# Mirrored rows of the second mixture go through a scratch in tile order, reversed by DRAM-to-DRAM copies

## The chip, the core and the metric

The kernel runs on one core of a Trainium2 chip. The metric is the device time of one execution in microseconds (us). The kernel before takes 789.74 us, the median of 3 runs (789.72 to 790.67).

Its engines are called PE (matrix multiply; PEld is its weight load), DVE (vector), ACT (scalar), POOL and SP. SP computes nothing here: it issues DMA transfers, in the order of the program.

## The reference, cut to what matters

```python
x = attn(x)                      # rfft along the sequence, complex mix, soft threshold, irfft
x = x + relu(norm(x)*g @ w11) @ w12          # first MLP, row by row
X = np.fft.fft(np.fft.fft(x, axis=1), axis=2)
u = x + np.real(X)                           # second mixture
out = u + relu(norm(u) @ w21) @ w22          # second MLP, row by row
```

There are 2 sequences (b = 0, 1) of 3136 rows of 256 fp32 channels; the MLPs are 1024 wide. Because x is real, row 3136 - n of `real(X)` is row n with its channels reversed (channel 256 - c in place of c). So one computed tile serves two sets of rows, the rows n and their mirror.

## The kernel before, in words

3136 rows are split as 49 x 64: row n = k1 + 49 * a, with k1 below 49 and a below 64. The first stages write the first mixture to DRAM, and 13 chunks of up to 512 rows (`mlp1`, the loop `run_mlp`) turn it into `dX1` in DRAM. A stage of 49-point transforms (`Stage98`) reads `dX1` as `u0r` and writes `dA2`. The second MLP (`mlp2`) has 13 chunks again, in the order of `plan2`: a chunk holds two pairs, such as k1 = 4 and 3 of sequence 0, and a pair fills two tiles of 128 rows. The first tile is the rows of k1 in its upper 64 partitions and those of k1 - 1 in its lower 64. The second is the mirrored rows: rows 3136 - k1 and 3136 - k1 + 1, and from each of them 64 rows backwards in steps of 49. The front of a chunk (`Front.stage_b`, `dmix`) computes real(X) for the first tile and adds it, reversed in the channels, to the second (L901, L904).

The rows of x that the tiles add to are loaded by `Chunk.fetch` (L660, `yb<-dX`), three chunks ahead. The results are stored by `Chunk.store` (L811, `out_dram<-o`). For a pair there are two loads of 64 rows and one of 128 mirrored rows, and as many stores. The access pattern of the mirrored ones is built in `chunks2`: in memory it is 2 x 64 rows of 1 KB, with a step of minus 49 rows inside.

Between norm and matmul the rows are transposed. `flip` transposes 32x32 blocks on DVE (L713) and writes them to DRAM (L719, `dT<-q`); `land` reads them back in the other order (L727, `q<-dT`); `trans` splits what came into two parts on ACT and DVE (L200 and L208, `u0r<-q`). This round trip of the next chunk happens while the present chunk is multiplied: `land` is asked for after the fourth of eight first-layer blocks (`LAND_AT`), behind the last store of the chunk before (`sent`), and `trans` at the first tile of the second layer.

The order on each engine is fixed when the program is built. All transfers but one go through SP's queue. Each DMA tells of its landing on one of eight counters, taken in turn (DMAHW0 to DMAHW7 in the order below), and SP issues a DMA only once the one that is eight before it has landed; such a wait holds up all that stands behind it. PE writes the second layer into two banks (`psb`), and DVE (L801, L802) frees a bank by adding it to the rows.

The lines of the change are those that build the mirrored access pattern in `chunks2` and the hooks ahead of the two calls of `run_mlp`; hooks are keyed by chunk, layer ("l1" or "l2") and step.

Of the kernel before, what the change touches and what calls it, by code (L numbers as in the profile page):

```python
# [9 lines left out]
F32 = mybir.dt.float32  # L10
# [27 lines left out]
LATE = {"b": (4, 6), "mix": (6, 7), "stats": (("l1", 7), ("l2", 0)), "norm": (("l2", 0),) * 4, "flip": (("l2", 2), ("l2", 3))}  # L38
LAND_AT = ("l1", 3)
PAD_AT = (15, 17)  # L40
TRANS1_AT = (4, 6)
PREP0_AT = (23, 24, 26, 28)
L2_BEHIND = 7
# [10 lines left out]
NB = 2  # L54
N = 3136
N1 = 49
N2 = 64
D = 256
NQ = 98
NK = 24  # L60
# [100 lines left out]
def fourier_moe_kernel(ctx, tc, x, w_r, w_i, b_r, b_i, g_ln, w11, w12, w21, w22,  # L161
                       t_ca, t_cam, t_cim, t_cb, t_ci, t_cb0, t_ci0, t_cd, t_ident, out):
    nc = tc.nc
    sp = nc.sync
# [3 lines left out]
    dp = ctx.enter_context(tc.tile_pool(name="dp", bufs=1, space=bass.MemoryType.DRAM))  # L168
# [36 lines left out]
    mark, tab, spx = {}, {}, {}  # L205
# [18 lines left out]
    def scratch(nm, n=NQ):  # L224
        return [dp.tile([n, FW], F32, name=f"{nm}{b}") for b in range(NB)]

    dY = [dp.tile([2, NQ, FW // 2], F32, name=f"dY{b}") for b in range(NB)]
    dX1, dA2 = scratch("dX1", 128), scratch("dA2", 128)

    def by_k1(t, k1, n):  # L230

        v = t.rearrange("q f -> (q f)")
        return v[(k1 - 1) * 32768:(k1 - 1 + n) * 32768].rearrange("(k p c) -> p k c", k=n, c=D)
# [584 lines left out]
    def chunks1(b, wv):  # L818
        cs = []
        if b == 0:  # L820
            plan = [(c * 512, 4) for c in range(6)]
        else:
            plan = [(64, 2), (320, 3)] + [(704 + c * 512, 4) for c in range(4)] + [(2752, 3)]
        for r0, nt in plan:
            lo = [(ALLP, 0, nt, half_rows(dY[b], r0, 128, nt))]
            st = [(ALLP, 0, nt, rows(dX1[b], r0, 128, nt))]
            if b == 1 and r0 == 64:
                for src, lst in ((dY, lo), (dX1, st)):
                    for h, (bb, rr) in enumerate(((0, 3072), (1, 0))):
                        lst.append((slice(h * 64, h * 64 + 64), nt, 1, half_rows(dY[bb], rr, 64, 1) if src is dY  # L830
                                    else rows(src[bb], rr, 64, 1)[:, 0, :]))
                nt += 1
            cs.append(Chunk(nt, lo, st, wv, True))
        return cs
# [71 lines left out]
    def chunks2(plan, wv):  # L906
        cs = []
        for pairs in plan:
            lo, st, nt = [], [], 0
            for pr in pairs:  # L910
                for src, lst in ((dX1, lo), (out, st)):
                    for h, (b, k1) in enumerate(pr):
                        v = src[b] if src is out else src[b].rearrange("q (j c) -> (q j) c", c=D)[0:N]
                        lst.append((slice(h * 64, h * 64 + 64), nt, 1,
                                    v.rearrange("(k a) c -> k a c", a=N1)[:, k1, :]))
                    if pr[0][1]:
                        b, k1 = pr[0]
                        assert pr[1] == (b, k1 - 1)
                        v = src[b]
                        m = bass.AP(v.tensor, v.offset + (N - k1) * D, [[D, 2], [-N1 * D, N2], [1, D]])  # L920
                        lst.append((ALLP, nt + 1, 1, m))
                nt += 2 if pr[0][1] else 1
            cs.append(Chunk(nt, lo, st, wv, False, Front(pairs)))
        return cs
# [84 lines left out]
    def l_pad(b):  # L1009

        sp.dma_start(out=dX1[b][NQ:128].rearrange("q (k f) -> q k f", k=8), in_=x[b].rearrange("k q f -> q k f")[0:128 - NQ])

    for b in range(NB):
        todo.setdefault(PAD_AT[b], []).append(lambda b=b: l_pad(b))
    mlp1 = chunks1(0, wv1) + chunks1(1, wv1)
# [168 lines left out]
    plan2 += [[((1, 4 * i + 4), (1, 4 * i + 3)), ((1, 4 * i + 6), (1, 4 * i + 5))] for i in range(5)]  # L1184
    plan2 += [[((1, 24), (1, 23))]]
    mlp2 = chunks2(plan2, wv2)


# [7 lines left out]
    def after(k, i, f):  # L1196

        def g():
            with tc.issue_after(mlp1[k].rest[i]):
                f()  # L1200
        return g

    def in_turn(chunks, k, f):

        def g():
            with tc.issue_after(chunks[k].pe):
                f()
        return g
# [15 lines left out]
    def store3(n, cs):  # L1224

        def g():
            with tc.issue_after(mlp1[n].trip):
                for c in cs:
                    inv[1].store(c)
        return g  # L1230

    def hook(k, part, i, f):
        hooks.setdefault((k, part, i), []).append(f)

    mlp2_w = load_mlp(w21, w22, r2b, "stg", True)
    hook(3, "l1", 5, mlp2_w[0])
    for (k, i), f in zip(MLP2_AT, mlp2_w[1:]):
        hook(k, "l1", i, after(k, i, f))
    for c, i in enumerate(TRANS1_AT):
        hook(0, "l1", i, in_turn(mlp1, 0, lambda c=c: mlp1[1].trans(c)))  # L1240
# [4 lines left out]
    hook(0, "l1", 0, l_cd)  # L1245
    hook(2, "l1", 3, store3(3, range(2)))
    hook(2, "l2", 2, store3(4, range(2, 4)))
    hook(*STAGE4_FROM[0], s4[0].start)
    hook(8, "l1", 1, after(8, 1, s4[0].ahead))
    hook(8, "l1", 6, in_turn(mlp1, 8, s4[0].middle2))  # L1250
# [6 lines left out]
    def ahead1():  # L1257
        with tc.issue_after(mlp2[2].applied), tc.issue_after(mlp2[0].pe):
            s4[1].ahead()

    hook(*STAGE4_FROM[1], s4[1].start)
    hook(0, "l2", 2, ahead1)
    hook(1, "l1", 2, in_turn(mlp2, 1, s4[1].middle2))
# [38 lines left out]
```

## Time and profile before

| | us |
|---|---|
| median of 3 runs | 789.74 |
| profiled execution | 789.01 |
| its span, first to last instruction | 787.1 |
| PE busy | 771.3 |
| weight loads (PEld) busy | 642.6 |
| DVE busy | 545.7 |
| ACT busy | 359.7 |
| transfers of SP's queue, share of 16 DMA engines | 43.2% |

The profiled execution is one run under the hardware profiler; the time outside its span is 1.9 us. A busy share is an average over stages, so it says where to look and not what an edit is worth. PE is busy in 98% of the span; PE's clock is granted in full except in one stretch around 510 to 521 us. The kernel moves 43% of what its DMA engines have time for, so in the mean they are not the limit; a single transfer can still be late.

### The profile page before, as it was taken

The page shows a single profiled execution, that of the slowest core. Times are in us where ns is not written, and L with a number is a line of the kernel's source. Part 1 is how long each engine was busy: PE and PEld are TensorE (multiplying, and loading weights), DVE is VectorE, ACT ScalarE, POOL GpSimd, SP SyncE. Part 2 cuts the span into 40 slices and gives each one's busy share as a digit, 9 for nine tenths or more (in the row PEclk, how much of TensorE's full clock was granted, in tenths as well). Part 3 has the DMA queues.
Part 4 walks back from the last instruction along what each step waited for, and adds up shares of the span by engine and source line. Part 5 has one row for each costly group of instructions (what it writes and reads, how often), then busy time and mean ns, then how long its engine had stood idle before and what let it go on. Part 6 is the DMA issues. An engine that isn't in the chain of part 4 may idle for free.

```text
span 787.1 us, 12213 instructions
## 1 busy us (share of the span) xinstructions
PE 771.3 (98%) x4396; PEld 642.6 (82%) x4396; DVE 545.7 (69%) x1253; ACT 359.7 (46%) x791; POOL 104.4 (13%) x113
## 2 busy tenths in 40 slices
PE   9999999999999999999999999789999999999997
PEld 3989978976788889977778988567788898888886
DVE  6799986886757988668667866446646667666643
ACT  0543366365654535536343244346534535444421
POOL 0564321330111001100000001324000000000000
PEclk9999999999999999999999999979999999999999
DMA  8853202613084333577862326555543334422211
GB/s 235 260 173 125 81 1 55 221 54 108 30 280 132 135 121 94 137 198 214 248 176 67 121 89 159 154 169 159 165 135 99 105 121 122 113 68 74 62 33 41
DMA packets 84706, 101.02 MB, mean 128 GB/s; under 512 B 20306, under 2 KB 63036, under 8 KB 84450
## 3 DMA queue, kind: packets, MB, share of 16 engines
q1 hardware_dynamic: 84566, 100.18, 43.2%
q8 instruction: 35, 0.57, 0.3%
q14 instruction: 25, 0.20, 0.1%
q10 hardware_dynamic: 80, 0.07, 0.0%
HBM read 60.76 MB, written 41.42 MB: 130 GB/s over the span
## 4 chain that ended last, share of the span: by engine, by line
PE 88%; DMA 4%; DVE 4%; issue 1%; ACT 1%; SPq 1%; POOL 0%; DVEq 0%; POOLq 0%; ACTq 0%
PE psb L795 22%; PE psb L796 11%; PE psa L218 11%; PE psa L220 11%; PE psa L219 11%; PE psb L520 7%; PE psc L337 4%; DMA q<-dT 4%; PE psc L867 2%; PE psa L487 2%; PE psc L542 2%; PE psa L324 2%; PE psc L892 1%; DMA yb<-dX 1%; PE psc L933 1%
## 5 line engine op out<-in xcount | busy, mean ns | idle before, releaser
L774 ACT ACTIVATE h<-psa 128x512 fp32r<-128x512 f32 (+2 forms) x208 | 117.8, 572 | 213.6 <-PE psa L220 160.3
L776 DVE SCALAR_TENSOR_TENSOR h<-psa,h 128x512 fp32r<-128x512 f32 (+2 forms) x208 | 134.8, 653 | 63.9 <-ACT h L774 60.4
L795 PE MATMUL psb<-r2b,h 128*128 128x512 f32 x392 | 138.9, 401 | 7.8 <-DVE o L802 7.8
L795 PE MATMUL psb<-r3a,h 128*128 128x512 f32 x392 | 137.6, 397 | 0.0
L796 PE MATMUL psb<-r2b,h 128*128 128x256 f32 x392 | 106.8, 283 | 0.0
L796 PE MATMUL psb<-r3a,h 128*128 128x256 f32 x392 | 106.5, 280 | 0.0
L795 PEld LDWEIGHTS psb<-r2b,h 128*128 128x128 f32 x392 | 73.0, 191 | 24.2 <-issue 8.5
L795 PEld LDWEIGHTS psb<-r3a,h 128*128 128x128 f32 x392 | 72.1, 188 | 20.8 <-issue 5.7
L520 PE MATMUL psb<-wm,h 128*128 128x256 f32 (+1 forms) x600 | 84.4, 290 | 0.0
L218 PE MATMUL psa<-u0r,r2b 128*128 128x512 f32 (+2 forms) x208 | 82.0, 394 | 1.1 <-ACT u0r L200 1.1
L520 PEld LDWEIGHTS psb<-wm,h 128*128 128x128 f32 (+1 forms) x600 | 76.6, 188 | 5.0 <-issue 3.2
L218 PE MATMUL psa<-u0r,r3a 128*128 128x512 f32 (+1 forms) x208 | 80.5, 387 | 0.0
L219 PE MATMUL psa<-u0r,r2b 128*128 128x512 f32 (+2 forms) x208 | 78.7, 378 | 0.0
L219 PE MATMUL psa<-u0r,r3a 128*128 128x512 f32 (+1 forms) x208 | 78.7, 378 | 0.0
L220 PE MATMUL psa<-u0r,r2b 128*128 128x512 f32 (+2 forms) x208 | 78.2, 381 | 0.0
L796 PEld LDWEIGHTS psb<-r2b,h 128*128 128x128 f32 x392 | 75.2, 192 | 3.1
L220 PE MATMUL psa<-u0r,r3a 128*128 128x512 f32 (+1 forms) x208 | 76.4, 378 | 0.0
L796 PEld LDWEIGHTS psb<-r3a,h 128*128 128x128 f32 x392 | 73.9, 189 | 2.6
L801 DVE TENSOR_TENSOR o<-psb,yb 128x256 f32<-128x256 f32 x74 | 30.1, 419 | 61.7 <-PE psb L796 61.1
L200 ACT ACTIVATE yg<-psc 128x512 f32<-128x512 f32 (+1 forms) x58 | 48.1, 869 | 41.0 <-PE psc L542 26.5
L218 PEld LDWEIGHTS psa<-u0r,r3a 128*128 128x128 f32 x208 | 39.0, 188 | 13.4 <-issue 5.7
L218 PEld LDWEIGHTS psa<-u0r,r2b 128*128 128x128 f32 x208 | 39.1, 188 | 13.0 <-issue 4.9
(119 smaller groups left out, 1191.9 us busy)
## 6 DMA issues: line engine op xcount, KB each, us to landing
dT<-q SPq DMA_DIRECT2D x19, 512.0 KB
q<-dT SPq DMA_DIRECT2D x19, 512.0 KB
s<-in_moe_w_ch_dram SPq DMA_DIRECT2D x16, 512.0 KB
u0r<-dX SPq DMA_DIRECT2D x32, 256.0 KB
dA<-o SPq DMA_DIRECT2D x64, 128.0 KB
dY<-yg SPq DMA_DIRECT2D x12, 512.0 KB
r<-dA SPq DMA_DIRECT2D x48, 128.0 KB
dX<-o SPq DMA_DIRECT2D x10, 512.0 KB
```

Of the source, the lines that this page charges most:

```text
L200: nc.scalar.activation(out=o, in_=i, func=AF.Copy, scale=scale)
L218: nc.tensor.matmul(out=ps, lhsT=lh, rhs=rh, start=first, stop=False)
L219: nc.tensor.matmul(out=ps, lhsT=ll, rhs=rh, start=False, stop=False)
L220: ins = nc.tensor.matmul(out=ps, lhsT=lh, rhs=rl, start=False, stop=last)
L324: ins = nc.tensor.matmul(out=ps, lhsT=cam, rhs=self.raw[g // 2][:, e * 512:(e + 1) * 512], start=True, stop=True)
L337: ins = nc.tensor.matmul(out=ps[s][64 * e:64 * e + 64, 0:n], lhsT=w[64 * s:64 * s + k], rhs=v[e][64 * s:64 * s + k], start=True, stop=True)
L520: ins = nc.tensor.matmul(out=ps[0:m, u * D:(u + 1) * D], lhsT=xv[:, o:o + m], rhs=wm_hl[wv][:, e, c, :], start=k == 0, stop=k == 11)
L774: ins = nc.scalar.activation(out=h[:, 0:n], in_=ps[:, 0:n], func=AF.Relu)
L776: ins = nc.vector.scalar_tensor_tensor(out=l[:, 0:n], in0=ps[:, 0:n], scalar=0.0, in1=h[:, 0:n], op0=ALU.max, op1=ALU.subtract)
L795: nc.tensor.matmul(out=ps, lhsT=h[:, ts_], rhs=w2[:, f, :], start=f == 0, stop=False)
L796: ins = nc.tensor.matmul(out=ps[:, 0:D], lhsT=l[:, ts_], rhs=w2[:, f, 0:D], start=False, stop=f == NF - 1)
L801: nc.vector.tensor_tensor(out=self.like(o), in0=self.like(ps[:, 0:D]), in1=self.y[:, i], op=ALU.add)
```

## The change

The mirrored rows no longer go between SBUF and their reversed places in DRAM. Four DRAM scratch tensors are added, `dM` for loads and `dO` for stores, one per sequence, of 24 x 64 rows each: row (m, a) is the mirrored row of k1 = 24 - m at place a, so the 128 rows of a mirrored tile lie one behind the other. A tile's load is one contiguous 128 x 1 KB read of `dM`, and its store one such write of `dO`. Eight DRAM-to-DRAM copies (`mirror_in`) fill `dM` from `dX1`, each 24 x 16 rows of 1 KB with the 16 rows going backwards in steps of 49. Eight more (`mirror_out`) take `dO` to `out`: four of 24 x 16 rows for sequence 0, four of 14 x 16 rows for sequence 1. Mirrored stores of sequence 1 with k1 above 14, five tiles, stay as they were (`DIRECT`). Every copy is issued by SP, behind whatever DMA it issued last at the hook's place.

```diff
+DIRECT = (1, 14)
+MIRROR_IN1 = ((3, 0, 48), (5, 0, 32), (6, 0, 16), (8, 0, 0), (10, 1, 48), (11, 1, 32), (12, 1, 16))
+MIRROR_IN2 = ((1, 1, 0),)
+MIRROR_OUT = ((7, "l1", 5, 0, 0), (7, "l2", 1, 0, 16), (8, "l1", 5, 0, 32), (8, "l2", 1, 0, 48),
+              (10, "l1", 5, 1, 0), (10, "l2", 1, 1, 16), (11, "l1", 5, 1, 32), (11, "l2", 1, 1, 48))
...
+    dM, dO = ([dp.tile([NK, N2 * D], F32, name=f"{nm}{b}") for b in range(NB)] for nm in ("dM", "dO"))
+    mir = lambda t, m, n: t[m:m + n].rearrange("m (a c) -> m a c", c=D)
+
+    def back_rows(t, m, n, a, w):
+        v = t.rearrange("q (j c) -> (q j) c", c=D) if t.shape[1] != D else t
+        return bass.AP(v.tensor, v.offset + (N - NK + m - N1 * a) * D, [[D, n], [-N1 * D, w], [1, D]])
+
+    def mirror_in(b, a, w):
+        ins = sp.dma_start(out=mir(dM[b], 0, NK)[:, a:a + w], in_=back_rows(dX1[b], 0, NK, a, w))
+        spx["ins"] = getattr(ins, "ins", ins)
+
+    def mirror_out(b, m, a, w):
+        ins = sp.dma_start(out=back_rows(out[b], m, NK - m, a, w), in_=mir(dO[b], m, NK - m)[:, a:a + w])
+        spx["ins"] = getattr(ins, "ins", ins)
...
-                        v = src[b]
-                        m = bass.AP(v.tensor, v.offset + (N - k1) * D, [[D, 2], [-N1 * D, N2], [1, D]])
+                        if src is out and (b, k1) > DIRECT:
+                            m = back_rows(src[b], NK - k1, 2, 0, N2)
+                        else:
+                            m = (dO if src is out else dM)[b].rearrange("m (a c) -> (m a) c", c=D)[(NK - k1) * N2:(NK - k1 + 2) * N2]
                         lst.append((ALLP, nt + 1, 1, m))
...
+    for k, b, a in MIRROR_IN1:
+        hook(k, "l1", 5, after_sp(mirror_in, b, a, 16))
...
+    for k, b, a in MIRROR_IN2:
+        hook(k, "l1", 5, after_sp(mirror_in, b, a, 16))
+    for k, part, i, b, a in MIRROR_OUT:
+        hook(k, part, i, after_sp(mirror_out, b, (0, NK - DIRECT[1])[b], a, 16))
```

On PE, DVE, ACT and POOL the instructions and their order are those of before. On SP there are 16 more DMAs, and a few have changed places. Two places of SP's queue follow; line numbers of the change are some 20 higher (L660 is L680, L719 is L739, L727 is L747, L811 is L831). In the names, `dX_68` and `dX_69` are `dX1` of sequence 0 and 1, the three `dT` are a ring, `r` is the front's tile, and a bracket names the counters that a DMA waits for.

SP before, in the second chunk of `mlp2`, from the round trip's write to its read:

```order
L719 DMA dT_192<-q 128x2x512 [waits DMAHW0_49,DVE_49]
L401 DMA u0r<-dX_69 64x1024 [waits DMAHW1_49]
L401 DMA u0r<-dX_69 64x1024 [waits DMAHW2_49]
L850 DMA r_5655<-dA_70 128x256 [waits DMAHW3_49,PE_49]
L850 DMA r_5655<-dA_70 128x256 [waits DMAHW4_49]
L660 DMA yb<-dX_68 64x256 [waits DMAHW5_49,DVE_49]
L811 DMA out_dram<-o 64x256 [waits DMAHW6_49,DVE_49]
L811 DMA out_dram<-o 64x256 [waits DMAHW7_49]
L660 DMA yb<-dX_68 64x256 [waits DMAHW0_49]
L660 DMA yb<-dX_68 128x1x256 [waits DMAHW1_49,DVE_49]
L811 DMA out_dram<-o 2x64x256 [waits DMAHW2_49,DVE_49]
L727 DMA q<-dT_192 128x8x128 [waits DMAHW3_49,Activation_49]
```

A mirrored load and a mirrored store stand right ahead of the read `q<-dT`. The same place in SP's queue in the change, without its first two rows, up to the first copy behind it:

```order
L421 DMA u0r<-dX_69 64x1024 [waits DMAHW1_49]
L870 DMA r_5667<-dA_70 128x256 [waits DMAHW2_49,PE_49]
L870 DMA r_5667<-dA_70 128x256 [waits DMAHW3_49]
L680 DMA yb<-dX_68 64x256 [waits DMAHW4_49,DVE_49]
L831 DMA out_dram<-o 64x256 [waits DMAHW5_49,DVE_49]
L831 DMA out_dram<-o 64x256 [waits DMAHW6_49]
L680 DMA yb<-dX_68 64x256 [waits DMAHW7_49]
L680 DMA yb<-dM_72 128x256 [waits DMAHW0_49,DVE_49]
L831 DMA dO_74<-o 128x256 [waits DMAHW1_49,DVE_49]
L747 DMA q<-dT_196 128x8x128 [waits DMAHW2_49,Activation_49]
L421 DMA u0r<-dX_69 64x1024 [waits DMAHW3_49]
L421 DMA u0r<-dX_69 64x1024 [waits DMAHW4_49]
```

Nothing has moved here; the mirrored load (128x1x256) and the mirrored store (2x64x256) have become plain ones, and the copy `dM_73<-dX_69` stands right behind these rows.

SP before, in the eighth chunk of `mlp2`, ahead of the write of the round trip:

```order
L660 DMA yb<-dX_69 64x256 [waits DMAHW5_49]
L811 DMA out_dram<-o 64x256 [waits DMAHW6_49,DVE_49]
L811 DMA out_dram<-o 64x256 [waits DMAHW7_49]
L811 DMA out_dram<-o 2x64x256 [waits DMAHW0_49,DVE_49]
L719 DMA dT_193<-q 128x2x512 [waits DMAHW1_49]
```

The mirrored store is the last one ahead of the write. The same place in SP's queue in the change:

```order
L680 DMA yb<-dX_69 64x256 [waits DMAHW6_49]
L831 DMA out_dram<-o 64x256 [waits DMAHW7_49,DVE_49]
L831 DMA out_dram<-o 64x256 [waits DMAHW0_49]
L831 DMA dO_75<-o 128x256 [waits DMAHW1_49,DVE_49]
L246 DMA out_dram<-dO_74 24x16x256 [waits DMAHW2_49]
L739 DMA dT_197<-q 128x2x512 [waits DMAHW3_49]
```

A copy of 384 rows now stands between the chunk's stores and the write of the round trip.

## Rows read from the trace of the kernel before

**Rows 1.** Page, part 1: busy us (share of the span) and instructions of each engine.
```profile
PE 771.3 (98%) x4396; PEld 642.6 (82%) x4396; DVE 545.7 (69%) x1253; ACT 359.7 (46%) x791; POOL 104.4 (13%) x113
```

**Rows 2.** PE's waits: engine line, what ended them, us in total, times, longest.
```profile
PE psb L795 <- DVE o L802: 7.8, 2, 7.7
...
PE psa L218 <- ACT u0r L200: 1.1, 1, 1.1
```

**Rows 3.** Stretches: us, then busy PE, PEld, DVE, ACT, POOL; PEclk, DMA share, GB/s.
```profile
220.00:340.00 120.00, 120.00 (x631) 104.84 (x630) 93.47 (x219) 58.75 (x129) 14.16 (x10) 1.00 0.50 151
500.00:521.00 21.00, 13.34 (x63) 10.64 (x62) 8.47 (x25) 6.78 (x18) 5.60 (x12) 0.76 0.49 135
519.00:521.00 2.00, 2.00 (x8) 1.70 (x8) 0.50 (x2) 0.00 (x0) 0.00 (x0) 0.58 0.53 179
521.00:545.00 24.00, 24.00 (x135) 18.00 (x134) 12.29 (x35) 13.02 (x32) 8.25 (x16) 1.00 0.72 211
```

**Rows 4.** Chain of work that ended last, 440 to 560 us: start, us, what.
```profile
445.68 9.82 DMA q<-dT
...
500.03 10.12 DMA q<-dT
...
514.98 0.76 PE psb L795
515.95 0.43 PE psb L795
516.59 0.43 PE psb L795
...
529.98 7.27 DMA yb<-dX
```

**Rows 5.** Timeline of SP's DMA issues, 484 to 502 us: start, us, what.
```profile
486.92 0.84 SPq L719 DMA_DIRECT2D dT<-q  x1
487.80 3.18 SPq L401 DMA_DIRECT2D u0r<-dX  x2
...
492.73 3.99 SPq L811 DMA_DIRECT2D out_dram<-o  x2
497.28 1.84 SPq L660 DMA_DIRECT2D yb<-dX  x2
499.37 0.56 SPq L811 DMA_DIRECT2D out_dram<-o  x1
500.03 1.67 SPq L727 DMA_DIRECT2D q<-dT  x1
```

**Rows 6.** Timeline of DVE, 488 to 492 us.
```profile
490.45 0.42 DVE L802 TENSOR_TENSOR o<-psb,o 128x256 f32<-128x256 f32 x1
```

**Rows 7.** Timeline of PE, 499 to 503 us: second-layer pairs at full clock.
```profile
500.52 0.39 PE L795 MATMUL psb<-r2b,h 128*128 128x512 f32 x1
...
500.86 0.40 PE L795 MATMUL psb<-r2b,h 128*128 128x512 f32 x1
```

**Rows 8.** Busy time by stretch: a lone mirrored store, then the DRAM-to-DRAM copy `dX<-in_x`.
```profile
748.50:750.50 2.00, 2.00 (x14) 1.72 (x13) 0.00 (x0) 0.00 (x0) 0.00 (x0) 1.00 0.13 42
60.00:62.00 2.00, 2.00 (x19) 2.00 (x18) 1.35 (x3) 0.53 (x1) 2.00 (x2) 1.00 0.94 352
```

**Rows 9.** DMA issues of mirrored rows: what, count, KB each.
```profile
yb<-dX SPq DMA_DIRECT2D x24, 128.0 KB
out_dram<-o SPq DMA_DIRECT2D x24, 128.0 KB
```

**Rows 10.** Timeline of SP: a read of the round trip at 663, a write at 674.
```profile
663.24 0.38 SPq L727 DMA_DIRECT2D q<-dT  x1
...
674.67 0.47 SPq L719 DMA_DIRECT2D dT<-q  x1
```

**Rows 11.** Timeline of ACT: the splits behind those round trips [idle before, releaser].
```profile
667.62 1.15 ACT L200 ACTIVATE u0r<-q 128x512 fp32r<-128x512 f32 x2 [2.12 <-DMA q<-dT]
...
692.40 1.15 ACT L200 ACTIVATE u0r<-q 128x512 fp32r<-128x512 f32 x2 [1.93 <-DMA q<-dT]
```

More of the change, by code (lines that the diff above doesn't have):

```diff
@@ L1230, in store3, with after_sp, g @@
         return g
+    def after_sp(f, *a):
+        def g():
+            with tc.issue_after(spx["ins"]):
+                f(*a)
+        return g
     def hook(k, part, i, f):
```

## The prediction, on record before the run

> **What bounds the kernel now.** I read the busy times first. PE is busy for 771.3 of 787.1 us [rows 1], so no change of transfers can be worth more than the 15.8 us in which PE idles, and what a slow clock costs. PE's waits come next: 7.8 us for DVE freeing a bank of `psb`, twice, once for 7.7 us, and 1.1 us for ACT's split `u0r` [rows 2]. The other idle time lies at the start, in waits that have to do with the first loads, and behind the last matmul. Then I looked for the place by stretches: from 220 to 340 us PE has no gap, from 500 to 521 us it works 13.34 of 21 us and its granted clock falls to 0.76 in the mean, and from 521 us on it is full again [rows 3]. So one place decides, and the chain of waits names it: the read `q<-dT` is issued at 500.03 us and takes 10.12 us, and PE starts again at 514.98 us [rows 4]. A second such read, at 445.68 us, takes 9.82 us; behind it is the wait of 1.1 us.
>
> How long should such a read take? One at 663.24 us ended the idle time of ACT at 667.62 us [rows 10, 11]: 4.4 us. Why the one at 500 us was late stands in SP's timeline [rows 5]. The read must follow the stores of the chunk before. DVE finished that chunk's last rows at 490.45 + 0.42 = 490.87 us [rows 6], but its stores were issued from 492.73 us on, the next loads at 497.28, the mirrored store at 499.37 and the read at 500.03. SP did not wait for DVE in these 9 us. It waited for counters: each DMA must wait for the one eight places before it, and among these are a mirrored store and a mirrored load ahead of the `dT<-q` of 486.92 us. How such transfers run is seen where one is alone: DMA share 0.13 of 16 engines, that is 2.1 engines, at 42 GB/s [rows 8]. So 128 KB (131 kB) take 3.1 us on two engines, and every transfer over all 16 that is queued behind them has to wait for its pieces on these two. The mirrored load issued at 529.98 us was waited for for 7.27 us [rows 4]. There are 24 such loads [rows 9] and 24 stores of the same shape.
>
> **The change part by part.** The instructions of four engines keep their order; only SP's queue changes.
>
> 1. All 24 mirrored loads and 19 of 24 stores become 128 rows of 1 KB one behind the other, as plain as the other loads. At the stall the order has the same rows, so the read now follows six DMAs after 490.87 us at most. At 0.6 us for an issue (the store of 499.37 took 0.56 [rows 5]) that is 494.5 us, and with 4.4 us for the read it lands at 498.9 us. It landed at 500.03 + 10.12 = 510.15 us, and from there to PE's restart took 514.98 - 510.15 = 4.8 us [rows 4]; PE ran dry 7.7 us before 514.98, at 507.3 [rows 2]; so the read has to land by 502.5 us. It does, with 3.6 us to spare. Gain: 7.7 us. The small wait in the same row, 0.1 us, has the same cause and goes too: 7.8 together.
>
> 2. The clock. It is full until the stall and at half of it (1.2 of 2.4 GHz) after: a pair of second-layer matmuls takes 516.59 - 515.95 = 0.64 us then [rows 4], and 500.86 - 500.52 = 0.34 us before [rows 7]. From 519 to 521 us the mean is 0.58, so half speed ends near 519 + 2 x 0.42 / 0.5 = 520.7 [rows 3]. From 514.98 to 520.7 PE did in 5.7 us what takes 5.7 x 0.34 / 0.64 = 3.0. Without the idle time before it, I take it that the clock doesn't fall: 2.7 us gained. If it falls all the same, 0.
>
> 3. The read of 445.68 us has two mirrored loads and the 512 KB store `dX<-o` right ahead of it in SP's queue. With the loads plain it should land 4.4 us after issue, or with that store ahead of it some 6 us, at 452. ACT waited for it until 455.5 and PE for 1.1 us: gain 1.1.
>
> 4. The copies are new. Eight of 384 rows in, four of 384 and four of 224 out: 12 x 393 kB + 4 x 229 kB = 5.6 MB. The nearest row is another DRAM-to-DRAM copy, with larger pieces, at 352 GB/s [rows 8]: 1.1 us for 393 kB. Pieces of 1 KB went at 42 / 2 = 21 GB/s on one engine, 336 on 16: 1.2 us. If a copy ran on two engines as the mirrored transfers do, it would take 9.4 us. So 1.1 to 9.4 us each; I take 1.2, since all these rows agree on the rate of one engine and the copies' outer step has 24 or 14 rows, not 2. They are issued behind the read of the round trip or ahead of its next write, and nothing needs their result for a chunk or more, but for the first out copies, whose stores are long done. I cost them at nothing on PE. What hides them is the slack of the round trip: the write of 674.67 us was used at 692.40 us, 17.7 us later [rows 10, 11], with no wait on PE; undisturbed, write and read need about 2 x 4.4 = 8.8. So a copy ahead of it may take 8.9 us before it is later than today.
>
> The Trainium skill's page "DMA: Bandwidth & Descriptors" (section "Why a DMA increments its semaphore by 16 and not by 1") says that a DMA runs on the largest number of engines up to 16 that divides the slowest dimension of both sides. By that rule a mirrored transfer of 2 x 64 rows has two engines, as the share of 0.13 shows, and a copy of 24 rows has 12, one of 14 rows 14: an estimate of 1.6 us for the larger, which changes the sum by nothing but makes 9.4 us unlikely; no run here shows it yet.
>
> 5. SP issues 16 more DMAs, about 0.6 us each, over some 550 us. Behind them on SP stand loads three chunks ahead; nothing.
>
> The end does not move: the last three chunks' mirrored stores stay direct.
>
> Sum: 7.8 + 2.7 + 1.1 = 11.6 us. The profiled execution takes 789.01 us, so 777.4; the median of the runs is 0.7 above it, at 789.74: 778.1 us. Next late is nothing on PE: ACT still waits 1.9 to 2.1 us for reads later on [rows 11] while PE is full.
>
> **The rivals.**
>
> A part of it only: the read at 500 us is late for other reasons too. For it: two loads `u0r` of 256 KB held SP for 3.18 us at 487.80, and more stand behind [rows 5]; the DMA engines' share is 0.49 there and 0.72 after [rows 3]. Against: most of the delay is counters, not bandwidth. If it lands halfway between 502.5 and 510.15, PE still idles 3.8 us and the clock falls: 3.9 + 0.1 + 1.1 = 5.1 us gained, 784.6 us.
>
> It does not do it: the counters are held by something else, such as those `u0r` loads, and the read stays where it is. 789.7 us, no difference.
>
> More than forecast: waits hidden within the matmul rows. From 521 to 545 us weight loads are busy for 18.00 of 24 us, 0.75, against 104.84 of 120, 0.87, where nothing disturbs [rows 3]. If that were lost time, 24 x (0.87 - 0.75) / 0.87 = 3.3 us more would come back: 774.8 us. Against: that stretch holds transforms of 512 columns for one load of 49 rows, so fewer loads are natural. The Trainium skill's page "Trainium Kernel Development and Optimization" (section "Performance Expectations") says that busy matmul time is a bad measure and weight loads a good one; by that rule this rival holds, and the trace bears it out little.
>
> Slower: a copy stands right ahead of the write `dT<-q`, as in the second pair of orders above, at four places. Its price is 0 until it takes 8.9 us, and from 8.9 + 11.6 / 4 = 11.8 us each the kernel is slower. That is above the upper bound of 9.4; with the copy also waiting for engines behind other transfers, say 13 us, it loses 4 x 4.1 = 16.4 against 11.6: 794.5 us.
>
> **How the numbers follow.** The forecast has 0.78, the part 0.10, more 0.03, no difference 0.04, slower 0.05. The forecast's own range is 777 to 780 us: 0.5 around the sum for the runs, and up to 2 for what small waits come up elsewhere. To hold 8 in 10 the range reaches into the part: 776.5 to 785. Faster and slower are counted from 0.2% (1.6 us), about what a measurement can tell here: faster 0.78 + 0.10 + 0.03 = 0.91, same 0.04, slower 0.05.
>
> **What would show it.** In the profile after, PE should be busy for some 768.6 us (771.3 less the 2.7 of the clock) in a span of 775.5 us, with no wait of more than 1 us for L802 (now L822), and a granted clock of 1.00 from 490 to 520 us. The read of the round trip should take 4 to 6 us in the chain or not appear there. A copy alone should show a DMA share well above 0.13. The forecast is wrong if PE still stops near 507 us, or if SP's waits for counters now name `dM` or `dO`.

## The result and the profile after

The changed kernel takes 777.11 us, the median of 4 runs (776.35 to 777.16), against 790.20 us (789.72 to 790.75, 4 runs) for the kernel before. The ratio is 0.983, with a 95% interval of 0.9815 to 0.9849. Forecast were 778.1 us and faster.

I read the profile after in the order of the prediction: busy times, PE's waits, stretches, chain, SP's queue. From the page of the changed kernel: its span and part 1 (engine, busy us, share of the span, instructions), its line on HBM (the DRAM), and part 4, the shares of the chain by engine:

```profile
span 775.3 us, 12224 instructions
PE 768.3 (99%) x4396; PEld 640.6 (83%) x4396; DVE 546.9 (71%) x1253; ACT 360.7 (47%) x791; POOL 104.5 (13%) x113
...
HBM read 66.40 MB, written 47.05 MB: 146 GB/s over the span
...
PE 94%; DVE 4%; issue 1%; ACT 0%; POOL 0%; DVEq 0%; POOLq 0%
```

PE has the same 4396 matmuls in 3.0 us less busy time [rows 1], which is matmuls at full instead of half clock, and the span is 11.8 us shorter. No DMA stands in the chain's shares any more; it was 4% before. The kernel reads 66.40 MB where the kernel before read 60.76, so 5.6 MB more, and writes as much more (47.05 against 41.42), as counted in step 4.

All of PE's waits in the changed kernel (line, what ended them, us in total, times, longest):

```profile
PE psc L955 <- POOL wz L951: 1.1, 1, 1.1
PE psc L223 <- DVE yg L346: 0.6, 1, 0.6
PE psc L566 <- POOL h L213: 0.5, 1, 0.5
PE psc L357 <- DVE mv L693: 0.4, 1, 0.4
```

Both rows of the waits shown of before [rows 2] are gone; the four that are left lie in the first 210 us and were there before, with the same times. The stretches of the changed kernel (us, busy PE, PEld, DVE, ACT, POOL, clock, DMA share, GB/s):

```profile
440.00:460.00 20.00, 20.00 (x120) 18.29 (x119) 17.07 (x50) 7.17 (x19) 0.00 (x0) 1.00 0.41 132
500.00:521.00 21.00, 20.86 (x121) 15.38 (x120) 10.41 (x26) 11.22 (x30) 8.17 (x15) 1.00 0.53 161
521.00:545.00 24.00, 24.00 (x139) 19.20 (x138) 15.44 (x41) 13.55 (x33) 8.01 (x16) 1.00 0.66 190
```

From 500 to 521 us PE now works 20.86 us, against 13.34 before, at a granted clock of 1.00 against 0.76 [rows 3]. Why shows in SP's timeline of the changed kernel (start, us, what), at the place of [rows 5]:

```profile
482.57 0.41 SPq L739 DMA_DIRECT2D dT<-q  x1
483.03 1.40 SPq L421 DMA_DIRECT2D u0r<-dX  x2
...
488.21 0.59 SPq L680 DMA_DIRECT2D yb<-dX  x1
489.20 0.33 SPq L680 DMA_DIRECT2D yb<-dM  x1
489.66 0.34 SPq L831 DMA_DIRECT2D dO<-o  x1
490.09 0.38 SPq L747 DMA_DIRECT2D q<-dT  x1
490.53 1.32 SPq L421 DMA_DIRECT2D u0r<-dX  x2
491.90 0.80 SPq L242 DMA_DIRECT2D dM<-dX  x1
```

The read `q<-dT` is issued 7.5 us after the write `dT<-q`, where it was 13.1 us [rows 5], and right behind the plain mirrored load and store; the copy follows it.

### The profile page after: what moved, and what is told of

Read it like the earlier page. It is cut to its first block, busy times and chain, and to the rows that moved or that the text cites. A ratio compares the mean times of both kernels' runs of the same rounds, so it can differ in the third digit from the quotient of the medians.

```text
span 775.3 us, 12224 instructions
## 1 busy us (share of the span) xinstructions
PE 768.3 (99%) x4396; PEld 640.6 (83%) x4396; DVE 546.9 (71%) x1253; ACT 360.7 (47%) x791; POOL 104.5 (13%) x113
## 3 DMA queue, kind: packets, MB, share of 16 engines
HBM read 66.40 MB, written 47.05 MB: 146 GB/s over the span
## 4 chain that ended last, share of the span: by engine, by line
PE 94%; DVE 4%; issue 1%; ACT 0%; POOL 0%; DVEq 0%; POOLq 0%
PE psb L815 24%; PE psa L223 12%; PE psb L816 12%; PE psa L225 11%; PE psa L224 11%; PE psb L540 7%; PE psc L357 4%; PE psc L887 3%; PE psa L507 2%; PE psc L562 2%; PE psa L344 2%; PE psc L912 1%; PE psc L955 1%; DVE h L213 0%; DVE w L547 0%
## 5 line engine op out<-in xcount | busy, mean ns | idle before, releaser
L815 PE MATMUL psb<-r2b,h 128*128 128x512 f32 x392 | 136.3, 396 | 0.1
L815 PEld LDWEIGHTS psb<-r2b,h 128*128 128x128 f32 x392 | 71.7, 188 | 15.9 <-PE psc L357 1.0
L816 PEld LDWEIGHTS psb<-r2b,h 128*128 128x128 f32 x392 | 73.9, 189 | 3.1
```

Source lines behind the costliest of these rows:

```text
L815: nc.tensor.matmul(out=ps, lhsT=h[:, ts_], rhs=w2[:, f, :], start=f == 0, stop=False)
L816: ins = nc.tensor.matmul(out=ps[:, 0:D], lhsT=l[:, ts_], rhs=w2[:, f, 0:D], start=False, stop=f == NF - 1)
```

## The experiments

My theory: the loss at 500 us came from transfers that run on two engines and hold up the round trip behind them. Rivals: the backward order of the rows costs; it is one half (loads or stores) that does it; the whole load on the DMA engines does it, not the place. In all seven kernels the order of instructions on PE, DVE, ACT and POOL is that of before. Spans and waits come from one profiled execution each, times are medians.

**Direction.** The kernel before, with the inner step forward; it leaves out the reversal of the rows in a mirrored tile.

```diff
-m = bass.AP(v.tensor, v.offset + (N - k1) * D, [[D, 2], [-N1 * D, N2], [1, D]])
+m = bass.AP(v.tensor, v.offset + (N - k1 - N1 * (N2 - 1)) * D, [[D, 2], [N1 * D, N2], [1, D]])
```

> The kernel before with the step inside the mirrored rows turned to plus 49: the same rows in forward order, still 2 x 64 rows a DMA. It leaves the reversal out (what is added to the mirrored rows belongs to other rows). Theory (two engines make these transfers slow, whatever the direction): no change, 790 us, the stall of 7 to 8 us near 507 us and the slow clock are there as before. Rival (reading and writing backwards is what is slow): the stall goes, 777 to 780 us.

Measured: 790.21 us, ratio 1.000 (0.9991 to 1.001). Its two waits and its stretch:

```profile
PE psb L795 <- DVE o L802: 8.0, 2, 7.6
PE psa L218 <- ACT u0r L200: 1.7, 2, 1.5
```
```profile
500.00:521.00 21.00, 13.40 (x68) 10.72 (x68) 9.29 (x25) 7.76 (x20) 6.83 (x14) 0.84 0.46 129
```

The stall and the fall of the clock are all there. In a transfer of 2 x 64 rows, going backwards costs nothing that these runs can tell.

**Engine count.** The same forward rows, but each mirrored transfer as two DMAs of 64 rows, which like the other 64-row loads have an outermost step of 64. No scratch, no copies; five stores (sequence 1, k1 above 14) stay whole. The reversal is left out again.

```diff
-    lst.append((ALLP, nt + 1, 1, m))
+    for h in range(2):
+        m = bass.AP(v.tensor, v.offset + (N - k1 + h - N1 * (N2 - 1)) * D, [[N1 * D, N2], [1, D]])
+        lst.append((slice(h * 64, h * 64 + 64), nt + 1, 1, m))
```

> The same forward order, but a mirrored load or store is two DMAs of 64 rows, as the plain ones are (the last five stores stay 2 x 64). No scratch, no copies; 43 more DMAs on SP. Theory: the stalls at 455 and 507 us go and the clock stays up, 777 us, as the change or up to 0.5 us better. Rival (the contiguous scratch, 128 rows in one DMA, is what matters): less than half of the gain, 784 us or more, since more DMAs take more of the eight counters.

Measured: 778.30 us, ratio 0.985 (0.9834 to 0.9863); no wait of PE for `o` or `u0r` stands in its list, and the clock is 1.00 throughout. That is 1.2 us above the 777 that I expected; 0.8 us of it, in the profiled execution, is a wait for input at the start. Against the run above only the split has changed, and with it the number of engines: the trace records each arrival that a DMA reports to its counter, and each half reports 16 of them where the whole reported 3. So the number of engines is the cause, and the scratch is one way to raise it. (Whether rows can go backwards on 16 engines without a scratch was not tried.)

**One half of the change.** Loads alone go through `dM`, with its eight copies, and stores stay as before:

```diff
+    if src is out:
+        m = back_rows(src[b], NK - k1, 2, 0, N2)
```

> The change with its loads alone: 24 mirrored loads from the scratch and eight copies in; the stores are those of before. Theory (what counts is whether the read of the round trip at 500 us lands by 502.5 us, and it has 3.6 us to spare with both gone): nearly all of the gain, 777 to 779.5 us, no wait over 1 us at 455 or 507. Rival (each transfer adds its share to one queue): half of it, 783 to 785 us.

Stores alone go through `dO`, with its eight copies, and loads stay as before:

```diff
+    if src is dX1 or (b, k1) > DIRECT:
+        m = back_rows(src[b], NK - k1, 2, 0, N2)
```

> The change with its stores alone: 19 mirrored stores to the scratch and eight copies out; the loads are those of before. Theory: the wait at 455 us, which has loads alone ahead of it, stays (1.1 us), the stall at 507 us goes or leaves up to 2 us: 778 to 781 us. Rival (shares): 784 to 786 us.

Measured: loads alone 777.53 us, ratio 0.984 (0.9825 to 0.9854), no stall; stores alone 781.48 us, ratio 0.990 (0.9878 to 0.9921). Waits of the stores-only kernel, its stretch, and its chain (start, us, what):

```profile
PE psb L815 <- DVE o L822: 2.0, 2, 1.6
PE psa L223 <- ACT u0r L205: 1.3, 2, 1.1
```
```profile
500.00:521.00 21.00, 19.43 (x111) 15.09 (x110) 11.21 (x30) 10.32 (x27) 7.71 (x15) 1.00 0.65 191
```
```profile
446.34 9.77 DMA q<-dT
...
497.63 7.39 DMA q<-dT
...
509.44 0.47 PE psb L815
```

The gains, 12.7 and 8.7 us, don't add up to the whole's 13.1: both halves cure the same stall, and either comes a long way. With only the stores plain, the read lands at 497.63 + 7.39 = 505.02 us, and PE starts again at 509.44, after a stop of 1.6 us. By that the deadline was here some 503.4 us, not the 502.5 of step 1: PE ran dry 0.5 us later than before, and started 4.4 us behind the landing, not 4.8. The time is 0.5 us above what I expected. With only the loads plain the read is early enough, and the stores on two engines cost nothing that can be measured. So the scratch for stores, with half of the copies, is not what the gain comes from: loads alone take 777.01 to 778.02 us, the whole change 776.35 to 777.16.

**The place alone.** In the kernel before, only the first chunk's two mirrored stores and the fourth chunk's two mirrored loads are split as above (forward; their reversal is left out).

```diff
-    lst.append((ALLP, nt + 1, 1, m))
+    if len(cs) == (0 if src is out else 3):
+        ... two DMAs of 64 rows, as above
```

> The kernel before, with only those mirrored transfers on 16 engines that stand around the stall: the two stores of the first chunk of the second MLP and the two loads of its fourth chunk, each as two DMAs of 64 rows in forward order (it leaves the reversal out for these four). The other 44 stay as before. Theory (the loss is one late round trip): the stall at 507 us and the slow clock go, the wait of 1.1 us at 455 us stays: 790.2 - 7.7 - 2.7 = 779.8 us, 779 to 781.5. Rival (the two-engine transfers cost everywhere a little): 784 us or more.

Measured: 783.63 us, ratio 0.992 (0.9905 to 0.9938): 6.1 us of the gain, less than I expected. The stall of 7.7 us is gone, but others are there. PE's waits, its chain, and its stretches:

```profile
PE psa L218 <- ACT u0r L200: 3.5, 2, 2.1
```
```profile
445.82 10.19 DMA q<-dT
...
531.70 7.16 DMA q<-dT
538.88 0.64 ACT u0r L200
539.56 0.50 PE psa L218
```
```profile
537.00:540.00 3.00, 0.93 (x10) 0.30 (x2) 0.46 (x1) 1.12 (x3) 1.98 (x5) 1.00 0.79 208
540.00:543.00 3.00, 3.00 (x9) 2.15 (x8) 2.18 (x5) 2.94 (x10) 1.98 (x3) 0.58 0.04 13
```

Each remaining stall is a read of the round trip queued behind mirrored loads that still run on two engines. The one at 445.82 us is that of before. The one at 531.70 was hidden by the big stall. In the kernel before, the chain has it as

```profile
538.46 7.73 DMA q<-dT
```

So it came 6.8 us later there, and took no less; but PE came some 10 us later (7.7 us of stall, 2.7 of slow clock), and had no wait for it. After the wait of 2.1 us the clock falls to 0.58 as well. Waits of 3.5 us and 770.2 - 768.3 = 1.9 us more busy time make 5.4 of the 5.9 us by which this span (781.2) is longer than the changed kernel's.

**The next places.** If that is so, the loads ahead of these two reads are all that is missing: the third and the sixth chunk's, together 8 of 48 transfers.

```diff
-    if len(cs) == (0 if src is out else 3):
+    if len(cs) in ((0,) if src is out else (2, 3, 5)):
```

> The kernel before, in which 8 of the 48 mirrored transfers run as two DMAs of 64 rows: the two stores of the first chunk and the two loads each of the third, fourth and sixth chunks. Those rows are taken in forward order (the reversal of the columns' rows is left out for them); no scratch, no copies; the other 40 transfers stay on two engines. Theory (a two-engine transfer costs only where a round trip is queued behind it while PE has no spare work; stall_only, with the fourth chunk's loads and the first's stores, still lost 1.6 us at 455 and 2.1 us with a drop of the clock at 537, each behind the read q<-dT queued after two mirrored loads): 777.5 to 779.5 us, no wait of PE over 1 us for u0r or o between 440 and 560 us, clock 1.00. Rival A (the stalls only move on to the next two-engine transfers, as the first of the fourth chunk moved to 537): 781 to 784 us, with a stall of over 1.5 us later than 540. Rival B (the gain is a matter of the whole load on the engines, and grows with the number of transfers changed): 8 of 48 give little more than 4 did, 782.5 to 784 us, spread over many small waits.

Measured: 778.49 us, ratio 0.986 (0.9843 to 0.9876). Waits, and the stretch of the last stall:

```profile
PE psc L938 <- POOL wz L934: 1.1, 1, 1.1
PE psc L218 <- DVE yg L326: 0.6, 1, 0.6
PE psc L546 <- POOL h L208: 0.5, 1, 0.5
PE psc L337 <- DVE mv L673: 0.4, 1, 0.4
PE psa L324 <- DMA h<-in_x_dram: 0.2, 1, 0.2
```
```profile
521.00:545.00 24.00, 24.00 (x137) 19.11 (x136) 15.05 (x41) 13.63 (x34) 8.28 (x17) 1.00 0.65 189
```

Its span is 775.8 us, 0.5 from that of the changed kernel, with 40 transfers still on two engines. So the gain sits in the few reads between 440 and 540 us and the transfers ahead of them, not in the mean load.

**The copies' cover.** In the changed kernel each copy of 24 rows is cut into 17 and 7 rows, to make the larger part slow. The lines show the copies in; those out for sequence 0 are cut alike, and the four copies of 14 rows stay whole.

```diff
-    ins = sp.dma_start(out=mir(dM[b], 0, NK)[:, a:a + w], in_=back_rows(dX1[b], 0, NK, a, w))
+    for m0, n in ((0, 17), (17, 7)):
+        ins = sp.dma_start(out=mir(dM[b], m0, n)[:, a:a + w], in_=back_rows(dX1[b], m0, n, a, w))
```

> The change, with its twelve copies of 24 x 16 rows cut into one of 17 x 16 and one of 7 x 16; 17 has no divisor up to 16 but 1, so the larger should run on one engine, 272 rows of 1 KB at 46 ns, 12.5 us. Theory (the copies are free while they stay shorter than the slack of the round trip, 8.9 us): late by some 4 us at several places, and loads of the front behind the copy at 492 us late by up to 12: 780 to 785 us. Rival (nothing waits for copies, at any price): 777 us, as the change. If every transfer behind a copy were held for its whole time: 800 us or more.

Measured: 786.87 us, ratio 0.996 (0.9946 to 0.9975), some 2 us above the top of what I expected. A stretch in which one copy runs almost alone, and the two around the new stall; PE's wait; SP's timeline; the chain:

```profile
700.00:705.00 5.00, 5.00 (x26) 4.21 (x26) 3.84 (x13) 2.54 (x6) 0.00 (x0) 1.00 0.07 25
...
710.00:717.00 7.00, 1.05 (x5) 0.75 (x4) 0.72 (x2) 1.15 (x2) 0.00 (x0) 0.74 0.29 83
717.00:725.00 8.00, 8.00 (x37) 6.72 (x36) 4.71 (x14) 4.56 (x12) 0.00 (x0) 0.80 0.28 93
```
```profile
PE psa L223 <- ACT u0r L205: 6.7, 2, 6.0
```
```profile
681.03 9.70 SPq L248 DMA_DIRECT2D out_dram<-dO  x2
690.83 1.59 SPq L682 DMA_DIRECT2D yb<-dX  x2
...
694.39 9.72 SPq L248 DMA_DIRECT2D out_dram<-dO  x2
704.22 0.45 SPq L741 DMA_DIRECT2D dT<-q  x1
```
```profile
704.22 7.30 DMA dT<-q
711.57 4.03 DMA q<-dT
715.62 0.64 ACT u0r L205
716.30 0.80 PE psa L223
```

A share of 0.07 is 1.1 of 16 engines. Such a pair of copies keeps SP itself for 9.7 us, most of it in the issue of the second copy, the one of 7 rows (8.91 us in the first pair shown and 7.80 in the other, where 1.2 us more are a wait for a counter). So the write behind them is issued at 704.22 us, then takes 7.30 us, and PE runs dry for 6.0 us, with a slower clock after. The place is that of the slower rival of the prediction; that SP itself is held is not in it. In the changed kernel the same copy holds SP for 0.82 us, and the write follows at once:

```profile
687.10 0.82 SPq L246 DMA_DIRECT2D out_dram<-dO  x1
688.01 0.48 SPq L739 DMA_DIRECT2D dT<-q  x1
```

## Why the prediction was right

**The whole.** A span of 775.3 us and PE busy for 768.3 stand where 775.5 and 768.6 were forecast. By the spans the gain is 787.1 - 775.3 = 11.8 us against the sum of 11.6. Of the 1.0 us by which 778.1 was too high, 0.7 is the distance of the median from the profiled execution, which I carried over and which was not there this time (777.13 and 777.11). So 777.11 lies at the lower end of the forecast's own range, 777 to 780.

**Step 1, the read at 500 us: right, with one link left out.** The read was forecast to be issued by 494.5 us and to land at 498.9; it was issued at 490.09 and landed at 495.6, after 5.5 us, inside the 4 to 6 forecast, and PE did not wait for it. A landing is the last arrival that a DMA reports to its counter. In the kernel before, the mirrored load of 486.28 us landed at 496.21, and the write `dT<-q` of 486.92 us behind it at 497.27, after 10.35 us. SP's waits between 480 and 512 us, in the kernel before, name both (us in total, times, longest):

```profile
SPq L811 <- DMA yb<-dX: 2.9, 1, 2.9
...
SPq L660 <- DMA dT<-q: 0.6, 1, 0.6
```

So SP waited for counters, as the prediction said. What it left out is that the write itself was late, and that the read stands on SP behind a load that waits for the write's counter, so it is never issued before the write has landed. In the changed kernel the write lands 3.1 us after its issue (482.57 to 485.6), and SP's waits in the same stretch name no DMA. The late write and the held counters both go back to the same mirrored transfers; no run separates them.

**Step 2, the clock: right in mechanism, 0.3 us small.** Forecast 2.7 us; PE's busy time fell by 771.3 - 768.3 = 3.0 us, and the clock is 1.00 from 500 to 521 us.

**Step 3, the read at 445 us: right.** It lands at 452.2 us, 6.4 after its issue, where 452 and some 6 were forecast, and appears in no wait of PE. It does with stores alone (1.1 us) and with the one place alone (3.5 - 2.1 = 1.4 us), where its loads stay on two engines.

**Step 4, the copies: hidden as said, their length wrong.** Forecast were 1.2 us each; the landings show 4.1 to 6.5 us from issue for the copies of 24 rows and 3.8 to 6.5 for those of 14. The forecast took the bytes alone; in the changed kernel even a 64 KB load `yb<-dX` takes 2.1 us at the least, so 1.2 was hardly to be expected. How much of the rest is engines shared with what goes on beside a copy is not shown. The lengths are within the bounds, and within the slack of 8.9 us. Of the share: near the end of one copy the changed kernel shows

```profile
724.10:724.70 0.60, 0.60 (x4) 0.52 (x3) 0.60 (x2) 0.12 (x1) 0.00 (x0) 1.00 0.41 143
```

with only that copy under way, so 6.6 engines in the mean of its last part, against 2.1 for a mirrored transfer [rows 8]. The number of arrivals tells more. It is one above the number of engines where the share tells that number: 3 for a mirrored transfer at 0.13, and 2 for a copy of 17 rows at 0.07. A copy of 24 rows reports 13, one of 14 rows 15; so they run on 12 and 14 engines. By the rule of the Trainium skill's page "DMA: Bandwidth & Descriptors" (section "Why a DMA increments its semaphore by 16 and not by 1"), the largest number up to 16 that divides the slowest dimension of both sides, these are the numbers to expect; the trace agrees, and the loss of 9.8 us by one cut shows what the rule is worth here.

**Step 5: right.** SP's issues of copies take 0.8 us, not 0.6, and nothing waits for them.

**The rivals.** "A part of it": the two `u0r` loads of 256 KB behind the write are still there and do not make the read late; they hold SP for 1.40 us now, against 3.18 before [rows 5]. "No effect": refuted by 13 us. "More than forecast": from 521 to 545 us weight loads rose from 18.00 to 19.20 us, but PE was busy for all 24 us before and after, and its whole busy time fell by the clock's 3.0 us alone. No hidden time came back. "Slower": its price came out near, by another road. Only two of its four places had a slow copy in the run on the copies' cover, those of sequence 0. With copies of 14 to 15 us (by their landings) it would say up to 2 x (15 - 8.9) = 12.2 us; by the spans 785.5 - 775.3 = 10.2 were lost, 9.7 of them waits of PE (6.7) and a busy time longer by 3.0. But the rival let the copy delay the write on the engines, and what the trace shows first is SP held in the issue. The writes were issued 9.5 us later than in the changed kernel at the first place (672.47 against 663.02) and 16.2 at the second (704.22 against 688.01), since the first delay runs on to the second. PE waited 0.7 and 6.0 us, so a slack of some 8.9 us was about right.

**The misses among the expectations.** I took the stall at 500 us for nearly the whole loss, and the sum's "next late is nothing" holds only because the change makes all mirrored loads plain at once. With one place mended, two more reads are late (1.4 and 2.1 us). The prediction did not look at the read at 538 us, so that the change cured it too was luck and not reasoning.

## What to carry to other kernels

Look at a transfer's DMA share where it is alone: 0.13 means two engines, and such a transfer, harmless for itself, can delay the full-width transfers queued behind it, here a write that took 10.4 us and takes 3.1 without them. A round trip through DRAM on the critical path is then worth more attention than the mean DMA load: eight plain transfers ahead of a few reads gave what 43 gave (778.5 and 778.3 us). When the first late wait is mended, go down the same queue for the next, which the first one hid.

## What the runs showed of the hardware

- In the profiled executions the clock did not fall at every wait: after the wait of 1.6 us at 507 us (stores alone) the stretch's mean is 1.00, after that of 2.1 us at 537 us (one place alone) 0.58 over the next 3 us, after 7.7 us half speed for 5.7 us of work. The same kernel can go either way: one of the four executions with stores alone took 784.39 us at a mean clock of 0.996, the others 781.2 to 781.7 at 0.999 to 1.000; and one of the four with one place alone had 1.000, the others 0.996 to 0.997, at much the same time.
- SP can be held by a DMA that it only issues: 7.80 and 8.91 us for a copy of 7 rows right behind one that runs on one engine, 0.82 us for the same 24 rows in one copy.
- Added work on DRAM costs nothing that these times show when it is in the right place: 5.6 MB of copies more, and the kernel is as fast as with 8 split transfers and no copies (spans 775.3 and 775.8 us).
